# When the first weights are loaded and converted in a fused attention and two-MLP kernel: order of the first loads, grain of v, one more conversion tile

## The chip, the cores and the metric

The kernel runs on one core of one Trainium2 chip. The metric is the time of one execution on the device in microseconds (us), as a median of several runs. Engines are named as in the profile: PE (TensorE; PEld is its weight load), DVE (VectorE), ACT (ScalarE), POOL (GpSimd) and SP (SyncE, which issues most DMAs).

## What is computed

Attention inside chunks of 64 positions (4 batches, 8 heads, 576 positions, 64 per head), then an MLP with squared ReLU, then a second MLP of four experts that are mixed by probabilities:

```python
scores = scale * np.matmul(q_c, k_c.transpose(0, 1, 2, 4, 3))
attn = np.exp(scores - max); attn = attn / (sum + 1e-09)
x = np.matmul(attn, v_c)                    # as 2304 tokens of 512
h = np.maximum(x @ w_in, 0.0)               # w_in 512 x 2048
x = h * h @ w_out                           # w_out 2048 x 512
h = np.maximum(x @ w1[e], 0.0)              # e = 0 to 3, 512 x 1024
out += p[:, e:e + 1] * (h @ w2[e])
```

`w_in` and `w_out` come as 64-bit floats, seen by the kernel as pairs of 32-bit words; everything else is 32-bit.

## The kernel before, in words

**Precision.** The MLP products take 32-bit operands as a rounded half (`hi`) and a remainder (`lo`): three matmuls for one product. So each weight tile and each tile of x is split by ACT (the rounding copy) and POOL or DVE (the subtraction).

**Ticks.** The order of all instructions is written out by hand: the loop over `r` (L659) records one tick after another, and each engine works through its own queue in that order. Tick r of the first 20 handles token tile r of 128 tokens (18 tiles) in a staggered way: scores of tile r on PE (`s1_stage`, L233) and their maxima and differences on DVE (L239, L240); the normalisation of tile r-1 on DVE (`norm_stage`, L251 to L254); the transposes of the attention weights of tile r-2 (`s2_stage`, L260), of q and of k of tile r+1 (`s0_stage`, L218, copied out by ACT at L222); the product with v for tile r-2 (`s3_stage`, L274) and its split into x (ACT L281, DVE L282). From tick 5 on (`LEAD`) the first MLP runs between these: step m = r-5 of `l1` (x @ w_in, 12 matmuls at L298, then ACT L308, DVE L309, ACT L311, DVE L312) and step m-1 of `l2` (12 matmuls at L328). A step takes one of four 128-wide pieces f of the hidden layer for one block of tokens; tiles 0 to 2 are the first block.

**Units.** A unit (n, which) is one 512 KB tile of `w_in` (which 0) or `w_out` (which 1) for piece n. It is loaded into one of four `raw` tiles (L108, L113), converted from 64 bits to 32 (ACT L125, L126; DVE L127, L130, and after a pause L135, L138; POOL L139, L140) into a tile `cv`, of which there are three (`CV_BUFS`), and split in a later tick (ACT L151, POOL L152), which frees the `cv` tile. `FIRST` gives the ticks in which the first eight units are converted, `FIRST_LOAD` those in which they are loaded; their order is (0,0), (1,0), (0,1), (2,0), (1,1), (3,0), (2,1), (3,1).

**Loads.** Before tick 0 the q, k of tiles 0 and 1 and two chunks of v are loaded, by SP and ACT. After that each tick's loads are recorded at its start: `do(r, "load")` calls each job, where a unit's load is issued at once, and `merge` takes the others (generators) in turn, one DMA of each. q and k of tile r+2 are due in tick r, v of batch b as a whole in tick 9b/2 - 1, on SP; k of tile 2 alone is issued by ACT. Each DMA takes the next of eight semaphores and waits for the transfer that last used that semaphore; the rows of the order below name them DMAHW0 to DMAHW7.

Of the kernel before, what the change touches and what calls it, by code (L numbers as in the profile page):

```python
# [13 lines left out]
ALU = mybir.AluOpType  # L14
# [11 lines left out]
LEAD = 5  # L26
QK_BUFS = 3
ACC_EARLY = 3
FIRST = [2, 3, 4, 4, 5, 6, 6, 7]
FIRST_LOAD = [0, 1, 2, 2, 3, 4, 5, 5]  # L30
WARM = 8
SECOND = [-3, -2, -1, 1, 2, 3, 4, 5]
RAW_BUFS = 4
CV_BUFS = 3
HALF = 384
NSUP = 3
SWAP = 63
# [9 lines left out]
def tile_kernel(ctx, tc, q, k, v, moe_w_in, moe_w_out, moe2_p, moe2_w1, moe2_w2, out):  # L47
    nc = tc.nc
# [3 lines left out]
    E, _, F2 = moe2_w1.shape  # L52
# [3 lines left out]
    NCB = S // CH  # L56
# [48 lines left out]
    def unit_load(n, which):  # L105
        r = rawp.tile([P, DM, 2], I32, tag="raw", name="raw")
        if which == 0:
            nc.sync.dma_start(  # L108
                out=r.rearrange("p (k f) w -> p k (f w)", k=KD),
                in_=moe_w_in[:, 2 * n * P:2 * (n + 1) * P].rearrange("(k p) f -> p k f", p=P),  # L110
            )
        else:
            nc.sync.dma_start(  # L113
                out=r.rearrange("p f w -> p (f w)"), in_=moe_w_out[n * P:(n + 1) * P, :]
            )
        raw[n, which] = r

    def unit_convert(n, which):

# [171 lines left out]
    def l1(i):  # L291
        p, tb, f = steps[i]
        T = BLOCKS[tb]
        ah, al = halves[p * G + f, 0]
        ph = bank("h" if "w" not in late else "httt")
        for kk in range(KD):
            for n, (w, x) in enumerate(((ah, xh), (ah, xl), (al, xh))):
                nc.tensor.matmul(  # L298
                    ph[:, :T], lhsT=w[:, kk, :], rhs=x[tb][:, kk, :],
                    start=(kk == 0 and n == 0), stop=(kk == KD - 1 and n == 2),  # L300
                )
            if kk < KD - 1:
                yield
        o = GP_AT + i % (LAG + 1) * 1024
        hi, lo = ar[:, o:o + 512], ar[:, o + 512:o + 1024]
        gh[i], gl[i] = hi, lo
        r = rp.tile([P, 512], F32, tag="r", name="r")
        nc.scalar.activation(out=r[:, :T], in_=ph[:, :T], func=AF.Relu)  # L308
        nc.vector.tensor_tensor(out=r[:, :T], in0=r[:, :T], in1=r[:, :T], op=ALU.mult)  # L309
        yield  # L310
        nc.scalar.copy(hi[:, :T], r[:, :T])  # L311
        nc.vector.tensor_tensor(  # L312
            out=lo[:, :T], in0=r[:, :T], in1=hi[:, :T].bitcast(F32), op=ALU.subtract
        )
# [251 lines left out]
    def at(tick, kind, fn, *args):  # L566
        jobs[kind].setdefault(max(0, tick), []).append((fn, args))

    def do(tick, kind):
        return [fn(*args) for fn, args in jobs[kind].pop(tick, ())]  # L570

    for t in range(2, NTILE):
        at(t - 2, "load", load_qk, t, (nc.sync, nc.scalar if t == 2 else nc.sync))
    for b in range(B):
        if b == 0:
            for c in (2, 3):
                at(0, "load", load_v_chunk, b, c, (nc.sync, nc.sync))
            at(1, "load", load_v, b, 4, NCB)
        else:
            at(b * NCB // 2 - 1, "load", load_v, b, 0, NCB)  # L580
    order = [(0, 0), (1, 0), (0, 1), (2, 0), (1, 1), (3, 0), (2, 1), (3, 1)]
    for p in range(npass1):
        for u, (f, which) in enumerate(order):
            if p == 0:
                tick = FIRST[u]
            elif p == 1:
                tick = NTILE + LAG_A + SECOND[u]
            else:
                tick = LEAD + (p - 1) * G * NB + UOFF[u]
            unit = (p * G + f, which)  # L590
            at(FIRST_LOAD[u] if p == 0 else tick - 2, "load", unit_load, *unit)
            at(tick, "convert", unit_convert, *unit)
            at(max(tick + 1, NTILE + LAG_A if p == 1 else 0), "split", unit_split, *unit)
    def merge(loads):
        loads = [y for y in loads if hasattr(y, "__next__")]
        while loads:
            loads = [y for y in loads if next(y, loads) is not loads]

    with tc.manual_schedule():
        ident = const.tile([P, P], F32, name="ident")  # L600
# [1 line left out]
        warm = bank("t")  # L602
        for _ in range(WARM):
            nc.tensor.matmul(warm[:, :P], lhsT=ident, rhs=ident, start=True, stop=True)
        two = (nc.sync, nc.scalar)
        merge([load_qk(0, two)])
        merge([load_qk(1, two)])
        for c in range(2):
            merge([load_v_chunk(0, c, two)])
        dp = const.tile([P, NTILE, E], F32, name="dp")  # L610
        psum_ = const.tile([P, NTILE, 1], F32, name="psum_")
        prob = const.tile([P, NTILE, E], F32, name="prob")
# [46 lines left out]
        for r in range(LEAD + NS + LAG):  # L659
            m = r - LEAD  # L660
            tags = "ttthaaaa" if m < 0 else "t"
            ch = mlp(m) if m >= 0 else iter(())
            if r == NTILE + LAG_A:
                att.close()
                late["x"] = ctx.enter_context(tc.tile_pool(name="xq", bufs=1, side="right"))
                late["w"] = lw.enter_context(tc.tile_pool(name="wpb", bufs=RING_B, side="right"))
            merge(do(r, "load"))
            if r < NTILE + LAG_A:
                if r < NTILE:
                    s1_stage(r, tags)  # L670
                if 0 <= r - 1 < NTILE:
                    norm_stage(r - 1)
                conv = do(r, "convert")
                for c in conv:
                    next(c)
                run(ch, 3)
                if 0 <= r - LAG_A:
                    s2_stage(r - LAG_A, tags)
                if r + 1 < NTILE:
                    s0_stage(r + 1, tags, 0)  # L680
                run(ch, 2)
                if r + 1 < NTILE:
                    s0_stage(r + 1, tags, 1)
                for c in conv:
                    run(c)
                run(ch, 1)
                if 0 <= r - LAG_A:
                    s3_stage(r - LAG_A, tags)
                if r < NTILE:
                    exp_stage(r)  # L690
                do(r, "split")
            else:
                if r == SWAP:
                    staging.close()
                    late["raw"] = ctx.enter_context(tc.tile_pool(name="raw", bufs=1, reuse_waits="tile"))
                for fn, args in early.pop(r, ()):
                    fn(*args)
                if r > y0_at:
                    next(late.setdefault("y0", y_combine(0)), None)
                if m < NS:  # L700
                    run(ch, KD + 2)
                    conv = do(r, "convert")
                    for c in conv:
                        next(c)
                    run(ch, 1)
                    for c in conv:
                        run(c)
                    do(r, "split")
            if m < NS:
                run(ch)  # L710
# [68 lines left out]
```

## Time and profile before

| | |
|---|---|
| median of 3 runs | 1264.28 us (1263.84 to 1265.97) |
| the profiled execution | 1261.85 us, span 1260.1 us |
| PE busy | 1231.7 us, 98% of the span |
| PEld busy | 1090.4 us, 87% |
| POOL busy | 628.8 us, 50% |
| DVE busy | 705.0 us, 56% |
| ACT busy | 521.3 us, 41% |
| PE in the first two of 40 slices | 6 and 7 tenths; 9 tenths in all others but the last |
| DMA in the first two of 40 slices | 209 and 197 GB/s; 68 GB/s over the span |

A busy PE is not a PE at its peak, since its matmuls are pipelined and their ends are modelled. The idle time of an engine counts only where the work that ended last ran through it: the chain of waits tells where that was.

### The profile page before, as it was taken

What the parts mean: (1) busy time and instruction counts of PE and PEld (TensorE: products, weight loads), DVE (VectorE), ACT (ScalarE), POOL (GpSimd) and SP (SyncE); (2) the same over time, 40 slices, a digit from 0 to 9 for tenths busy, and PEclk for the clock granted to TensorE, in tenths of its full rate; (3) what the DMA queues carried; (4) which work ended last, traced back from release to release, by engine and by line L of the source; (5) the groups of instructions that cost most, each with busy time, mean ns of one, the idle gap of its engine ahead of it and who ended that gap; (6) DMA issues with size and microseconds to landing.
All of it is one profiled execution on the core that took longest, in us unless ns stands there. A gap on an engine that the chain in (4) does not pass through costs nothing.

```text
span 1260.1 us, 18090 instructions
## 1 busy us (share of the span) xinstructions
PE 1231.7 (98%) x7048; PEld 1090.4 (87%) x7048; DVE 705.0 (56%) x1135; ACT 521.3 (41%) x934; POOL 628.8 (50%) x507
## 2 busy tenths in 40 slices
PE   6799999999999999999999999999999999999998
PEld 5688788988988988888888888888888888888887
DVE  4876667755765355355555573555555735555555
ACT  3654455432432223633333355333333553333331
POOL 0530046431432022766776686767766866666650
PEclk7889999999999999999999999999999999999999
DMA  9947012210201000222222223222222232222211
GB/s 209 197 77 168 5 51 87 66 51 17 67 1 50 1 1 17 67 67 68 67 67 67 68 76 109 68 69 70 69 69 70 66 122 68 70 67 69 67 35 66
DMA packets 136838, 87.19 MB, mean 69 GB/s; under 512 B 62769, under 2 KB 120113, under 8 KB 136753
## 3 DMA queue, kind: packets, MB, share of 16 engines
q1 hardware_dynamic: 133088, 85.12, 24.9%
q10 hardware_dynamic: 3664, 0.92, 0.4%
q8 instruction: 55, 0.90, 0.3%
q14 instruction: 31, 0.25, 0.1%
HBM read 81.30 MB, written 4.72 MB: 68 GB/s over the span
## 4 chain that ended last, share of the span: by engine, by line
PE 91%; DVE 3%; ACT 1%; issue 0%; POOL 0%; DVEq 0%
PE psa L543 32%; PE pst L498 24%; PE psa L328 14%; PE pst L298 9%; PE psh L298 6%; PE psh L498 4%; PE pst L274 1%; PE pst L233 1%; PE pst L218 1%; DVE cv L127 0%; PE pst L260 0%; DVE r L309 0%; DVE cv L130 0%; DVE ar L312 0%; DVE cv L135 0%
## 5 line engine op out<-in xcount | busy, mean ns | idle before, releaser
L543 PE MATMUL psa<-ar 128*128 128x512 f32 x1728 | 445.7, 393 | 0.0
L543 PEld LDWEIGHTS psa<-ar 128*128 128x128 f32 x1728 | 320.0, 188 | 50.3
L466 POOL TENSOR_TENSOR ar<-raw,ar 128x896 fp32r<-128x896 f32 x96 | 204.2, 2129 | 274.4 <-ACT ar L465 274.4
L498 PE MATMUL pst<-ar 128*128 128x384 f32 x1728 | 339.2, 335 | 0.9 <-ACT u L507 0.9
L498 PEld LDWEIGHTS pst<-ar 128*128 128x128 f32 x1728 | 307.3, 188 | 22.8 <-ACT u L507 1.6
L556 DVE SCALAR_TENSOR_TENSOR o<-psa,prob,o 128x512 f32<-128x512 f32 x270 | 201.5, 747 | 173.4 <-PE psa L543 173.4
L139 POOL TENSOR_TENSOR raw<-raw 128x512 f32<-128x512 f32 x32 | 36.2, 1131 | 230.0 <-DVE raw L138 97.6
L456 POOL TENSOR_TENSOR raw<-raw 128x256 f32<-128x256 f32 x192 | 141.3, 754 | 8.8 <-DMA raw<-in_moe_w 5.2
L475 POOL TENSOR_TENSOR ar<-raw,ar 128x512 fp32r<-128x512 f32 x96 | 123.4, 1306 | 12.5 <-ACT ar L474 12.5
L309 DVE TENSOR_TENSOR r<-r 128x512 f32<-128x512 f32 (+1 forms) x80 | 64.9, 811 | 108.9 <-ACT r L308 108.8
L328 PE MATMUL psa<-ar 128*128 128x512 f32 (+1 forms) x480 | 114.7, 379 | 1.3 <-POOL ar L152 1.2
L507 ACT COPY u<-pst 128x384 f32<-128x384 f32 x96 | 46.0, 479 | 163.8 <-PE pst L498 163.8
L511 ACT ACTIVATE ar<-pst 128x384 fp32r<-128x384 f32 x96 | 47.2, 492 | 149.7 <-DVE pst L532 116.3
L328 PEld LDWEIGHTS psa<-ar 128*128 128x128 f32 x480 | 87.6, 191 | 14.3 <-POOL ar L152 1.5
L328 PE MATMUL psa<-ar,h 128*128 128x512 f32 (+1 forms) x320 | 93.7, 373 | 1.6 <-ACT ar L311 0.8
L511 ACT ACTIVATE ar<-psh 128x384 fp32r<-128x384 f32 x96 | 47.2, 492 | 109.8 <-DVE psh L521 78.6
L465 ACT CAST ar<-raw 128x896 fp32r<-128x896 f32 x96 | 90.1, 939 | 0.0
L312 DVE TENSOR_TENSOR ar<-r,ar 128x512 fp32r<-128x512 f32 (+1 forms) x80 | 61.6, 770 | 39.9 <-ACT ar L311 39.1
L512 DVE SCALAR_TENSOR_TENSOR ar<-psh,ar 128x384 fp32r<-128x384 f32 x96 | 53.5, 558 | 53.6 <-ACT ar L511 53.6
L311 ACT CAST ar<-r 128x512 fp32r<-128x512 f32 (+1 forms) x80 | 46.1, 577 | 71.0 <-DVE r L309 71.0
L512 DVE SCALAR_TENSOR_TENSOR ar<-pst,ar 128x384 fp32r<-128x384 f32 x96 | 53.5, 557 | 31.2 <-ACT ar L511 29.1
L298 PE MATMUL pst<-ar,h 128*128 128x512 f32 (+1 forms) x240 | 69.3, 370 | 0.0
(106 smaller groups left out, 1482.9 us busy)
## 6 DMA issues: line engine op xcount, KB each, us to landing
raw<-in_moe_w SPq DMA_DIRECT2D x48, 512.0 KB, 3.9
raw<-in_moe_w SPq DMA_DIRECT2D x48, 256.0 KB, 3.0
raw<-in_moe_w SPq DMA_DIRECT2D x96, 128.0 KB, 3.0
raw<-in_moe_w_in SPq DMA_DIRECT2D x16, 512.0 KB, 3.8
raw<-in_moe_w_out SPq DMA_DIRECT2D x16, 512.0 KB, 3.7
out<-o SPq DMA_DIRECT2D x18, 256.0 KB, 3.2
q<-in_q SPq DMA_DIRECT2D x16, 256.0 KB, 4.7
v<-in_v SPq DMA_DIRECT2D x24, 144.0 KB, 4.5
```

Of the source, the lines that this page charges most:

```text
L298: nc.tensor.matmul(ph[:, :T], lhsT=w[:, kk, :], rhs=x[tb][:, kk, :], start=(kk == 0 and n == 0), stop=(kk == KD - 1 and n == 2),)
L309: nc.vector.tensor_tensor(out=r[:, :T], in0=r[:, :T], in1=r[:, :T], op=ALU.mult)
L328: nc.tensor.matmul(o, lhsT=w, rhs=y, start=(f == 0 and n == 0), stop=(f == G - 1 and n == 2))
L456: nc.gpsimd.tensor_tensor(out=r[:, o], in0=r[:, a], in1=r[:, b], op=op)
L465: nc.scalar.copy(h, a)
L466: nc.gpsimd.tensor_tensor(out=l, in0=a, in1=h.bitcast(F32), op=ALU.subtract)
L475: nc.gpsimd.tensor_tensor(out=l, in0=a, in1=h.bitcast(F32), op=ALU.subtract)
L498: nc.tensor.matmul(p, lhsT=w[:, kk, :], rhs=y[:, kk, :], start=(kk == 0 and z == 0 and u in (0, 1, 3)), stop=(kk == 1 and z == 2 and u in ...
L511: nc.scalar.activation(out=h, in_=p, func=AF.Relu)
L512: nc.vector.scalar_tensor_tensor(out=l, in0=p, scalar=0.0, in1=h.bitcast(F32), op0=ALU.max, op1=ALU.subtract)
L543: nc.tensor.matmul(p, lhsT=w[:, ts], rhs=y[:, i, :], start=(i == 0 and z == 0), stop=(i == 1 and z == 2))
L556: nc.vector.scalar_tensor_tensor(out=o, in0=p, scalar=pe, in1=o, op0=ALU.mult, op1=ALU.add)
```

## The change

Six edits; line numbers in the changed kernel are higher by 3 to 9.

1. Units (0,0) and (1,0) are loaded by SP before tick 0, between q of tile 0, q of tile 1 and v.
2. Unit u of the first eight is converted in tick u (before: 2, 3, 4, 4, 5, 6, 6, 7), split in the tick after, and loaded in tick u-2.
3. A unit's load becomes a generator too, and `run_all` issues the loads of a tick one job after the other instead of in turns: q and k, then v, then the unit.
4. v of batch 0 comes chunk by chunk (two chunks a tick), v of the others in two parts, four chunks and five, each later by one tick or more. SP issues k of tile 2.
5. There are four `cv` tiles instead of three.
6. The square in `l1` is computed by DVE as max(ph, 0) * r from the PSUM tile `ph` and ACT's result r, instead of r * r.

```diff
-FIRST = [2, 3, 4, 4, 5, 6, 6, 7]
-FIRST_LOAD = [0, 1, 2, 2, 3, 4, 5, 5]
+FIRST = [0, 1, 2, 3, 4, 5, 6, 7]
-CV_BUFS = 3
+CV_BUFS = 4
...
+    def unit_load_later(n, which):
+        unit_load(n, which)
+        yield
...
-        nc.vector.tensor_tensor(out=r[:, :T], in0=r[:, :T], in1=r[:, :T], op=ALU.mult)
+        nc.vector.scalar_tensor_tensor(
+            out=r[:, :T], in0=ph[:, :T], scalar=0.0, in1=r[:, :T], op0=ALU.max, op1=ALU.mult
+        )
...
-        at(t - 2, "load", load_qk, t, (nc.sync, nc.scalar if t == 2 else nc.sync))
+        at(t - 2, "load", load_qk, t)
     for b in range(B):
         if b == 0:
-            for c in (2, 3):
-                at(0, "load", load_v_chunk, b, c, (nc.sync, nc.sync))
-            at(1, "load", load_v, b, 4, NCB)
+            for c in range(2, NCB):
+                at(c // 2 - 1, "load", load_v_chunk, b, c, (nc.sync, nc.sync))
         else:
-            at(b * NCB // 2 - 1, "load", load_v, b, 0, NCB)
+            at(b * NCB // 2, "load", load_v, b, 0, NCB // 2)
+            at((b * NCB + NCB // 2) // 2, "load", load_v, b, NCB // 2, NCB)
...
-            at(FIRST_LOAD[u] if p == 0 else tick - 2, "load", unit_load, *unit)
+            if tick > 1:
+                at(tick - 2, "load", unit_load_later, *unit)
...
-    def merge(loads):
-        loads = [y for y in loads if hasattr(y, "__next__")]
-        while loads:
-            loads = [y for y in loads if next(y, loads) is not loads]
+    def run_all(loads):
+        for y in loads:
+            if hasattr(y, "__next__"):
+                for _ in y:
+                    pass
...
-        merge([load_qk(0, two)])
-        merge([load_qk(1, two)])
-        for c in range(2):
-            merge([load_v_chunk(0, c, two)])
+        run_all([load_qk(0, two)])
+        unit_load(*order[0])
+        run_all([load_qk(1, two)])
+        unit_load(*order[1])
+        run_all([load_v_chunk(0, c, two) for c in range(2)])
...
-            merge(do(r, "load"))
+            run_all(do(r, "load"))
```

The DMA queue of SP from its start, before (`in_moe_w_in` and `in_moe_w_out` are units; a q or k tile is 128x8x64, a v chunk two DMAs of 64x4x64):

```order
L184 DMA q<-in_q 128x8x64 x2
L207 DMA v<-in_v 64x4x64 x2
L108 DMA raw<-in_moe_w_in 128x4x256
L184 DMA q<-in_q 128x8x64
L207 DMA v<-in_v 64x4x64 x4
L108 DMA raw<-in_moe_w_in 128x4x256
L184 DMA q<-in_q 128x8x64
L196 DMA v<-in_v 64x5x64 x2
L184 DMA k<-in_k 128x8x64
L196 DMA v<-in_v 64x5x64 x6
L113 DMA raw<-in_moe_w_out 128x1024
L108 DMA raw<-in_moe_w_in 128x4x256
```

And in the changed kernel, up to the unit that tick 1 loads:

```order
L187 DMA q<-in_q 128x8x64
L107 DMA raw<-in_moe_w_in 128x4x256
L187 DMA q<-in_q 128x8x64
L107 DMA raw<-in_moe_w_in 128x4x256
L210 DMA v<-in_v 64x4x64 x2
L187 DMA q<-in_q 128x8x64
L187 DMA k<-in_k 128x8x64
L210 DMA v<-in_v 64x4x64 x4
L112 DMA raw<-in_moe_w_out 128x1024
L187 DMA q<-in_q 128x8x64
L187 DMA k<-in_k 128x8x64
L210 DMA v<-in_v 64x4x64 x4
```

Two units now stand ahead of v and one of them ahead of q of tile 1; q and k of a tile stand together, and the rest of v no longer lies between them.

The queue of ACT in ticks 0 and 1, before, with the semaphores that each row waits for (L222 copies q and k, L246 is the exponential, L125 opens a conversion):

```order
L222 COPY kT<-pst 128x512 [waits PE_49]
L184 DMA k<-in_k 128x8x64 [waits DMAHW0_49]
L222 COPY qT<-psa 128x512 [waits PE_49]
L222 COPY kT<-psa 128x512 [waits PE_49]
L246 ACTIVATE e<-e 128x512 [waits DVE_49]
L222 COPY qT<-pst 128x512 [waits PE_49,Activation_49]
```

And in the changed kernel (L225 and L249 are those lines, L128 opens a conversion):

```order
L225 COPY kT<-pst 128x512 [waits PE_49]
L128 ACTIVATE cv<-raw 128x512 [waits DMAHW3_49]
L129 ACTIVATE raw<-raw 128x512
L225 COPY qT<-psa 128x512 [waits PE_49]
L225 COPY kT<-psa 128x512 [waits PE_49]
L249 ACTIVATE e<-e 128x512 [waits DVE_49]
L128 ACTIVATE cv<-raw 128x512 [waits DMAHW7_49]
L129 ACTIVATE raw<-raw 128x512
L225 COPY qT<-pst 128x512 [waits PE_49,Activation_49]
```

The issue of k of tile 2 has left ACT's queue. In its place, ahead of the copies of tile 1, stands the first conversion, which waits for unit (0,0); the second stands ahead of the copies of tile 2.

## Rows read from the trace of the kernel before

**Rows 1.** By stage: stretch, length, busy PE, PEld, DVE, ACT, POOL; clock, DMA share, GB/s.

```profile
0.00:2.00 2.00, 0.66 (x3) 0.66 (x4) 0.00 (x0) 0.00 (x0) 0.68 (x6) 1.00 0.03 8
...
20.00:40.00 20.00, 12.82 (x222) 11.37 (x224) 17.60 (x41) 11.83 (x22) 6.25 (x6) 0.84 1.08 205
40.00:58.00 18.00, 13.59 (x149) 12.23 (x146) 15.55 (x30) 9.99 (x20) 11.03 (x9) 0.84 0.97 220
90.00:500.00 410.00, 408.18 (x2464) 352.83 (x2461) 244.16 (x390) 161.74 (x291) 113.82 (x86) 1.00 0.16 45
```

**Rows 2.** The chain of waits, 0 to 160 us: start us, us, what.

```profile
74.94 1.49 PE psh L298 x7
...
76.86 0.44 PE pst L218 x4
...
81.67 0.91 PE pst L233 x30
...
89.74 0.91 PE pst L233 x30
```

**Rows 3.** ACT in order of time: start us, us, what, idle before and its releaser.

```profile
11.27 0.58 ACT L222 COPY qT<-psa 128x512 f32<-128x512 f32 x1 [4.30 <-DMA raw<-in_moe_w_in]
```

**Rows 4.** Who waited for whom, 0 to 76 us: us in total, times, longest.

```profile
ACT cv L125 <- POOL ar L152: 14.4, 4, 6.1
```

**Rows 5.** The same for DVE alone, 9.7 to 75.3 us.

```profile
DVE mx L239 <- PE psa L233: 4.3, 1, 4.3
...
DVE r L309 <- ACT r L308: 2.1, 2, 1.0
DVE ar L312 <- ACT ar L311: 2.0, 2, 1.3
```

**Rows 6.** DVE in order of time, ticks 3 and 4.

```profile
27.45 0.68 DVE L251 TENSOR_REDUCE sm<-e 128x8 f32<-128x512 f32 x1
...
29.22 0.42 DVE L127 TENSOR_SCALAR cv<-cv 128x512 f32<-128x512 f32 x1
...
30.13 0.69 DVE L135 SCALAR_TENSOR_TENSOR cv<-raw,cv 128x512 int32<-128x512 int32 x1
30.86 0.43 DVE L138 TENSOR_SCALAR raw<-cv 128x512 int32<-128x512 int32 x1
32.86 0.69 DVE L282 TENSOR_TENSOR ar<-psa,ar 128x512 fp32r<-128x512 f32 x1 [1.58 <-ACT ar L281]
33.47 0.41 DVE L239 TENSOR_REDUCE mx<-psa 128x4 f32<-128x256 f32 x1
...
35.05 0.68 DVE L251 TENSOR_REDUCE sm<-e 128x8 f32<-128x512 f32 x1
```

**Rows 7.** DVE's squares (L309; min/median/max ns) and an operation like the new one (L512).

```profile
L309 DVE TENSOR_TENSOR r<-r x80: 546/691/1779, 48.7 to 499.2; 128x512 f32<-128x512 f32 x48, 128x384 f32<-128x384 f32 x32
...
L512 DVE SCALAR_TENSOR_TENSOR ar<-psh,ar 128x384 fp32r<-128x384 f32 x96 | 53.5, 558 | 53.6 <-ACT ar L511 53.6
```

**Rows 8.** DVE and POOL in order of time, tick 5.

```profile
51.60 1.29 POOL L140 TENSOR_TENSOR cv<-cv,raw 128x512 f32<-128x512 f32 x1
...
51.66 1.65 DVE L312 TENSOR_TENSOR ar<-r,ar 128x384 fp32r<-128x384 f32 x1 [0.72 <-ACT ar L311]
```

**Rows 9.** PE in order of time, ticks 4 to 6.

```profile
37.51 0.65 PE L218 MATMUL pst<-ident,k 128*128 128x128 f32 x4 [3.44 <-DMA k<-in_k]
...
39.07 1.53 PE L233 MATMUL pst<-kT,qT 64*64 64x64 f32 x31
41.99 3.25 PE L298 MATMUL psh<-ar 128*128 128x384 f32 x9 [1.38 <-DVE ar L282]
...
50.12 1.83 PE L298 MATMUL psh<-ar 128*128 128x384 f32 x9
```

**Rows 10.** Busy time by stage, the stretch of half clock in tick 5.

```profile
39.10:45.90 6.80, 5.42 (x52) 5.13 (x47) 6.57 (x12) 1.62 (x3) 6.05 (x5) 0.50 1.11 239
```

**Rows 11.** POOL's longest operation of a conversion: ns min/median/max, first and last start.

```profile
L140 POOL TENSOR_TENSOR cv<-cv,raw x8: 1282/1301/1371, 26.6 to 72.4; 128x512 f32<-128x512 f32 x8
```

## The prediction

> **What bounds the kernel now.** I read the stages first. From 90 us on PE is busy 408.18 of 410 us at full clock [rows 1]; before that it is not: 12.82 of 20 us between 20 and 40 us, 13.59 of 18 between 40 and 58, at a mean clock of 0.84, while DVE works 17.60 of 20 and 15.55 of 18 us and the DMA share is about 1 at 205 to 220 GB/s. So there are two kernels: a start in which PE waits, and a rest in which PE sets the time. The chain of waits puts the border at 74.94 us: from there on it is PE without a gap, and the ticks follow each other at 89.74 - 81.67 = 8.07 us [rows 2]. Whatever makes tick 9 begin earlier than 81.67 us (its first scores on PE) is carried to the end, because everything behind is PE's own work. That one number is what I forecast.
>
> Three things hold the start back. ACT stood 4.30 us before the copies of tile 1, behind the issue of k of tile 2, which waited for the first unit's transfer [rows 3]; DVE stood 4.3 us for tile 1's scores in consequence [rows 5]. ACT waited 14.4 us in four pieces, up to 6.1 us, to begin a conversion, because all three `cv` tiles were taken until POOL had split one [rows 4]; behind that stand the copies of q and k, ReLU and cast of the same tick, and DVE waited 2.1 and 2.0 us for the last two [rows 5]. And in tick 5 PE ran at half clock: 5.42 us of work between 39.1 and 45.9 us [rows 10], where nine matmuls took 3.25 us that take 1.83 at full clock [rows 9].
>
> **The change, part by part.**
>
> *k of tile 2 leaves ACT, conversions move to ticks 0 to 7.* The 4.30 us stop goes. In its place ACT waits for unit (0,0) ahead of tile 1's copies, and so on tick by tick. A unit that tick r converts stands in the DMA queue ahead of q of tile r+1, whose copies it precedes on ACT, so it is there first and costs ACT only its two instructions. What is late next is the transfer itself. Bytes ahead of a tile's end: 0.524 MB for each tile's q and k, 0.524 for each unit, 0.131 for each chunk of v. Tile 5 ends after 6 tiles, 5 units and 8 chunks, 6.81 MB; at 0.205 MB/us [rows 1] and a start at 2 us (up to then next to nothing moves [rows 1]) that is 35.2 us, against k of tile 5 at 37.51 us now [rows 9]. Tile 8 ends after 9 tiles, 8 units and 13 chunks, 10.6 MB: 53.8 us. From k's arrival to tile 5's scores were 39.07 - 37.51 = 1.6 us [rows 9], and the scores take 0.9 [rows 2]: DVE can take up tile 5 at 35.2 + 2.5 = 37.7 us. By then five conversions lie behind it instead of four.
>
> *Ticks 5 to 7.* DVE's work in a tick, from [rows 6]: scores 35.05 - 33.47 = 1.58; normalisation 29.22 - 27.45 = 1.77; conversion 30.13 - 29.22 = 0.91 and 30.86 + 0.43 - 30.13 = 1.16; x 33.47 - 32.86 = 0.61. The square is 0.55 at its shortest [rows 7], and I take the same for the remainder. Sum 7.1 us. POOL's conversions run beside it: L312 began 0.06 us after L140 of POOL and took 1.65 us, ending 0.42 us after POOL's end, 1.1 more than its shortest [rows 8]. I add 0.7 a tick, between nothing and that. So 7.8 us in tick 5, and in ticks 6 and 7 PE's pace of 8.07 is the longer one. DVE takes up tile 6 at 45.5, tile 7 at 53.6, tile 8 at 61.7 us; transfers are ahead from tile 6 on. In tick 8 PE's q transposes wait for the first half of the scores on DVE (0.8), and from there to tick 9 are 81.67 - 76.86 = 4.81 us [rows 2]: tick 9 at 67.3 us.
>
> *Clock.* PE still idles in ticks 1 to 4, so I keep one stretch of 6.8 us at half clock on the path, as in tick 5 now [rows 10]: 3.4 us. Bounds: none, or two of them. Tick 9 at **70.7 us, 11.0 us earlier**.
>
> *Four `cv` tiles.* Now a `cv` tile is written again four units later, when its split is two ticks old: the 14.4 us of [rows 4] go. This is what lets ticks 5 to 7 run at the sum above. If the cover went (POOL more than two ticks behind), the wait of up to 6.1 us would be back.
>
> *v in chunks and halves.* 26 more DMAs on SP, 2 for batch 0 and 8 for each other batch; later units are also moved past q, k and v of their tick. Nobody waits for SP in the chain of waits. v is loaded two ticks before it is used, 16 us at 8.07 a tick, and a unit likewise: nothing. If that cover were gone, PE would stop for what is missing of one transfer in a tick.
>
> *The square from PSUM.* 558 ns for an operation of that kind and size against 546 at the shortest now [rows 7]: nothing in the start; later the mean falls, off the path. PE's next step must now wait until DVE has read `ph`, where ACT's ReLU sufficed: a rival.
>
> **Sum.** The profiled execution took 1261.85 us, so 1261.85 - 11.0 = 1250.9; the median of the runs stands 2.4 above it, which gives **1253.3 us**. Ends: no half clock, and transfers at 220 GB/s [rows 1] (tile 5 at 33.0, 2.2 earlier): 1247.7. Half clock twice: 1256.7.
>
> **Rivals.**
>
> *The units stop ACT after all.* The eight semaphores make each DMA wait for the eighth before it, so a unit can be issued late; then ACT stands before the copies as it did once, for 4.3 us [rows 3]. Once on the path: 1257.6. For it: two units now precede v of tile 0, and the transfers are full. Against it: the order puts each unit ahead of the tile that it could stop.
>
> *The one bank of `ph`.* Until tick 19 there is one PSUM bank for `l1`. If PE waits 0.5 us for DVE's square in each of 15 ticks, 7.5 us go: about 1261. It decides where DVE lags the tick by more than the PE work between two steps; in a tick the second layer's twelve matmuls, two transposes and two attention products lie between, so I give it little.
>
> *POOL holds DVE up (slower).* POOL's three operations on a unit take up to 1.3 us each [rows 11], 3.9 a tick, now in every tick from 0 to 8. If each held DVE up for its whole length, a tick would be 3.2 us longer than I reckon; in ticks 2 to 7 that is 19.2 us, tick 9 at 89.9, slower than now: **1272.5**. The point from which it decides: 0.7 + 11.0 / 6 = 2.5 us lost a tick. For it speaks [rows 8]; against it that this row shows 1.1 us in the tick with the longest such operation. The Trainium skill, page "SBUF — State Buffer", section "SBUF: two separate sides", says that DVE and GpSimd share one pair of ports as an exclusive lock, that a DVE instruction needs it with two SBUF inputs or in a 2-port mode, and that the loser blocks for the whole instruction. By it this rival would be the upper end, and the new square, with one input in PSUM, would be out of it. The trace agrees as far as L312 ended 0.42 us after POOL did; no row shows what share of POOL's operations meets such an instruction.
>
> *It changes nothing.* Tiles no earlier and DVE as late as now: 1264. Against it: both ACT stops end by construction.
>
> **How the numbers follow.** Forecast 0.62 (1248 to 1257), units stop ACT 0.16, one bank 0.09, POOL 0.06, nothing 0.04, earlier than my low end 0.03. Range 1247.5 to 1260: it takes in the forecast's ends and the first rival and leaves out about 0.2. A measurement of this kernel can tell 0.2%, 2.5 us, from no change: faster 0.86 (forecast, first rival, low end, half of the bank's), within 0.2% 0.08, slower 0.06.
>
> **What would show it.** In the changed profile ACT should not wait for a `cv` split (now 14.4 us) nor 4 us for a unit; DVE should take up tile 5 near 38 us and tile 8 near 62 to 65; the scores of tick 9 should begin on PE at 67 to 74 us, the ticks behind it last 8.07 us. Wrong would be: ACT waits of several us for units; DVE operations beside POOL over 1 us in every tick; PE idle before `l1`'s first matmul for DVE's square; or a start shorter by 11 us and a time that is not, which would mean that the rest is not PE's alone.

## The result and the profile after

The changed kernel takes **1248.32 us** (median of 4 runs, 1247.99 to 1248.79) against 1264.23 us (1263.84 to 1265.97, 4 runs beside it): ratio 0.9877 [0.9865, 0.9889], 15.9 us faster. Forecast were 1253.3 us in a range of 1247.5 to 1260. The profiled execution took 1248.07 us, its span is 1246.2 us, 13.9 less than before.

Line numbers are those of the changed kernel now: scores L236, their maxima and differences L242 and L243, normalisation L254 to L257, transposes L221, conversions L128 and L129 (ACT), L130 to L141 (DVE), L142 and L143 (POOL), splits L154 and L155, x L284 and L285, `l1` L301, ReLU L311, square L312, its split L316 and L317, `l2` L333.

Busy time by stage, the stretches of [rows 1], columns as there:

```profile
20.00:40.00 20.00, 14.09 (x225) 11.68 (x224) 19.21 (x39) 12.31 (x23) 10.82 (x10) 0.76 0.94 199
40.00:58.00 18.00, 17.34 (x215) 15.83 (x214) 16.76 (x37) 12.55 (x24) 9.98 (x8) 1.00 0.78 177
90.00:500.00 410.00, 407.77 (x2377) 352.95 (x2376) 227.00 (x382) 163.50 (x290) 114.90 (x91) 1.00 0.16 45
```

PE is fuller between 40 and 58 us (17.34 of 18 us instead of 13.59), at full clock. Between 20 and 40 us DVE is: 19.21 of 20. The chain of waits (start us, us, what), where [rows 2] showed tick 9 at 81.67:

```profile
27.94 6.70 DMA k<-in_k
34.65 0.04 issue
...
48.17 0.63 PE pst L221 x4
...
69.23 0.91 PE pst L236 x30
...
77.32 0.91 PE pst L236 x30
```

k of tile 5 lands at 34.65 us. From 48.17 us on the chain is PE's alone, where before it was from 74.94. Tick 9 begins on PE at 69.23, 12.4 us earlier; the ticks behind are as long as before (77.32 - 69.23 = 8.09, then 7.93). The weight loads of the second MLP's first layer (min/median/max ns, then first and last start in us), in the kernel before:

```profile
L498 PEld LDWEIGHTS pst<-ar x1728: 186/188/189, 500.9 to 1247.5; 128*128 128x128 f32 x192
```

and in the changed kernel:

```profile
L503 PEld LDWEIGHTS pst<-ar x1728: 186/188/189, 487.0 to 1233.6; 128*128 128x128 f32 x192
```

So 13.9 us are won there: 12.4 up to tick 9, and 1.5 between tick 9 and the end of the first MLP. From there on the two run alike (1247.5 - 500.9 = 746.6 us and 1233.6 - 487.0 = 746.6 us).

Some of ACT's waits from 0 to 76 us (the longest and the one for units), where [rows 4] had 14.4 us for `cv` tiles and [rows 3] 4.30 for a unit:

```profile
ACT aT L265 <- PE pst L263: 7.3, 4, 2.4
...
ACT kT L225 <- PE pst L221: 4.1, 5, 2.0
...
ACT cv L128 <- DMA raw<-in_moe_w_out: 0.9, 2, 0.6
```

No wait for a split is left, and for units ACT waits 0.9 us in all. DVE's waits from 9.7 to 75.3 us, against [rows 5]:

```profile
DVE ar L317 <- ACT ar L316: 2.1, 4, 0.8
DVE mx L242 <- PE psa L236: 1.6, 1, 1.6
DVE ar L285 <- ACT ar L284: 1.5, 1, 1.5
```

DVE in order of time in tick 4 (start us, us, what), and beside it POOL:

```profile
32.36 0.42 DVE L242 TENSOR_REDUCE mx<-psa 128x4 f32<-128x256 f32 x1
...
33.94 0.68 DVE L254 TENSOR_REDUCE sm<-e 128x8 f32<-128x512 f32 x1
34.65 0.97 DVE L255 TENSOR_SCALAR sm<-sm 128x8 f32<-128x8 f32 x1
...
36.50 0.42 DVE L130 TENSOR_SCALAR cv<-cv 128x512 f32<-128x512 f32 x1
...
39.09 0.42 DVE L242 TENSOR_REDUCE mx<-pst 128x4 f32<-128x256 f32 x1
```

```profile
34.33 1.26 POOL L155 TENSOR_TENSOR ar<-cv,ar 128x512 fp32r<-128x512 f32 x1
```

DVE has no pause in this tick. Its addition on 8 columns (L255) lasts 0.97 us and ends at 35.62, right behind POOL's split at 35.59; free of POOL it takes 172 ns.

When DVE takes up each tile (first L242 of it, L239 in the kernel before, us) shows where each kernel gains or loses. The last two columns are the start of tick 9 on PE, from the chain of waits, and the time of the profiled execution. The experiments in the rows are told further below; e7 and e11 carry the main finding.

| tile | 1 | 2 | 3 | 4 | 5 | 6 | 7 | 8 | tick 9 | time |
|---|---|---|---|---|---|---|---|---|---|---|
| before | 14.04 | 19.93 | 25.87 | 33.47 | 41.85 | 53.23 | 63.24 | 75.22 | 81.67 | 1261.85 |
| after | 13.37 | 18.71 | 25.61 | 32.36 | 39.09 | 47.20 | 54.54 | 63.26 | 69.23 | 1248.07 |
| e3, old v | 12.36 | 18.76 | 25.08 | 36.34 | 42.28 | 50.43 | 57.76 | 66.48 | 72.45 | 1251.36 |
| e4, k2 on ACT | 16.70 | 22.03 | 28.94 | 35.69 | 42.43 | 53.24 | 60.56 | 69.27 | 75.24 | 1254.17 |
| e7, edits 1 to 3 | 16.42 | 21.76 | 28.66 | 35.40 | 42.18 | 52.22 | 59.54 | 68.25 | 74.21 | 1254.45 |
| e9, fill | 13.41 | 18.75 | 27.24 | 33.22 | 39.94 | 48.06 | 55.38 | 64.10 | 70.07 | 1248.98 |
| e10, pairs | 13.24 | 18.58 | 25.49 | 30.25 | 38.63 | 47.85 | 57.70 | 65.76 | 71.70 | 1250.73 |
| e11, old ticks | 12.43 | 18.48 | 24.41 | 30.35 | 39.55 | 50.67 | 60.54 | 69.89 | 77.87 | 1256.65 |
| e12, POOL remainder | 13.27 | 18.65 | 25.99 | 32.28 | 39.03 | 46.15 | 55.27 | 63.20 | 70.20 | 1248.68 |

The gain is not made while the first tiles arrive: at tile 4 it is 1.1 us. It is made from there on: ticks 5 to 7 of the kernel before were 3.3, 2.7 and 3.3 us longer. Against the changed kernel, e3, e4, e9, e10 and e11 lose in the time what they lose by the start of tick 9, within 0.2 us (e12 0.4 less, and e7, with the old square, 1.4 more); so what decides lies ahead of tick 9. A start is not the same twice: two kernels that differ from the changed one only later on, e2 and e8, take up tile 1 at 12.1 us instead of 13.37, and yet begin tick 9 at 69.25 and 69.30.

### The profile page after: what moved, and what is told of

The parts are those of the page before. It is cut to its first block, busy times and chain, and to the rows that moved or that the text cites. A ratio compares the mean times of both kernels' runs of the same rounds, so it can differ in the third digit from the quotient of the medians.

```text
span 1246.2 us, 18128 instructions
## 1 busy us (share of the span) xinstructions
PE 1228.4 (99%) x7048; PEld 1088.0 (87%) x7048; DVE 687.5 (55%) x1135; ACT 522.7 (42%) x934; POOL 621.7 (50%) x507
## 4 chain that ended last, share of the span: by engine, by line
PE 94%; DVE 3%; DMA 1%; ACT 1%; issue 0%; SPq 0%; DVEq 0%; ACTq 0%
PE psa L548 32%; PE pst L503 24%; PE psa L333 15%; PE pst L301 9%; PE psh L301 6%; PE psh L503 4%; PE pst L277 1%; PE pst L221 1%; PE pst L236 1%; DMA q<-in_q 1%; DMA k<-in_k 1%; PE pst L263 0%; DVE cv L130 0%; DVE cv L133 0%; DVE cv L138 0%
## 5 line engine op out<-in xcount | busy, mean ns | idle before, releaser
L142 POOL TENSOR_TENSOR raw<-raw 128x512 f32<-128x512 f32 x32 | 33.3, 1041 | 228.3 <-issue 103.9
L512 ACT COPY u<-pst 128x384 f32<-128x384 f32 x96 | 46.0, 479 | 163.7 <-PE pst L503 163.7
L333 PE MATMUL psa<-ar 128*128 128x512 f32 (+1 forms) x480 | 112.8, 375 | 0.1
L333 PEld LDWEIGHTS psa<-ar 128*128 128x128 f32 x480 | 86.3, 188 | 12.6 <-DVE ar L317 0.4
L333 PE MATMUL psa<-ar,h 128*128 128x512 f32 (+1 forms) x320 | 93.2, 372 | 1.1 <-ACT ar L316 0.8
L317 DVE TENSOR_TENSOR ar<-r,ar 128x512 fp32r<-128x512 f32 (+1 forms) x80 | 60.6, 757 | 39.4 <-ACT ar L316 37.8
L312 DVE SCALAR_TENSOR_TENSOR r<-pst,r 128x512 f32<-128x512 f32 (+1 forms) x48 | 30.7, 640 | 71.2 <-ACT r L311 71.2
L311 ACT ACTIVATE r<-pst 128x512 f32<-128x512 f32 (+1 forms) x48 | 26.7, 557 | 102.8 <-PE pst L301 102.1
L301 PE MATMUL pst<-ar,h 128*128 128x512 f32 (+1 forms) x240 | 69.3, 370 | 0.0
```

Source lines behind the costliest of these rows:

```text
L301: nc.tensor.matmul(ph[:, :T], lhsT=w[:, kk, :], rhs=x[tb][:, kk, :], start=(kk == 0 and n == 0), stop=(kk == KD - 1 and n == 2),)
L317: nc.vector.tensor_tensor(out=lo[:, :T], in0=r[:, :T], in1=hi[:, :T].bitcast(F32), op=ALU.subtract)
L333: nc.tensor.matmul(o, lhsT=w, rhs=y, start=(f == 0 and n == 0), stop=(f == G - 1 and n == 2))
```

## Experiments

Each changed kernel is compared with runs of the kernel before on the same chip, so the ratios stand beside 0.9877 [0.9865, 0.9889].

### e1: three `cv` tiles

```diff
-CV_BUFS = 4
+CV_BUFS = 3
```

> The changed kernel with three cv tiles again. Theory A, that of the prediction: the fourth tile is what lets ticks 5 to 7 run; then ACT waits for POOL's splits again (14.4 us of such waits before) and the time goes back by 3 to 8 us, to 1251 to 1256. Theory B: the waits came from ticks with two conversions (4 and 6); with one a tick, unit u needs the tile of unit u-3, whose split is recorded two ticks earlier, so nothing waits and the time stays within 1 us of 1248.3.

Measured: 1248.57 us, ratio 0.9885 [0.9872, 0.9899], the time of the changed kernel. ACT waits for no split here either. That is theory B: the fourth tile carries nothing once conversions are early and one to a tick.

### e2: the old square

```diff
-        nc.vector.scalar_tensor_tensor(
-            out=r[:, :T], in0=ph[:, :T], scalar=0.0, in1=r[:, :T], op0=ALU.max, op1=ALU.mult
-        )
+        nc.vector.tensor_tensor(out=r[:, :T], in0=r[:, :T], in1=r[:, :T], op=ALU.mult)
```

> The changed kernel with the square as r * r again. Theory A: the 1.4 us that the changed kernel gains behind tick 9 (PE's waits for DVE's remainder and the order around 185 to 215 us) come from the shorter, undisturbed square: 1249 to 1250.5. Theory B: the square is off the path everywhere: 1248.3 within 0.7, and the 1.4 us belong to loads or to POOL.

Measured: 1249.84 us, 0.9898 [0.9883, 0.9913]; by the times alone this hardly differs from the changed kernel. The trace places it: tick 9 begins on PE at 69.25 us (69.23 after), and the second MLP begins 1.6 us later than after:

```profile
L501 PEld LDWEIGHTS pst<-ar x1728: 186/188/189, 488.6 to 1235.2; 128*128 128x128 f32 x192
```

So the square is what wins the 1.5 us behind tick 9 (theory A). PEld's largest waits for the split of the square between 76 and 490 us in this kernel (`l2` is L331 here):

```profile
PEld psa L331 <- DVE ar L315: 2.1, 5, 0.6
PEld psa L331 <- ACT ar L314: 1.7, 3, 1.2
```

In the changed kernel they are 1.2 us each (69 to 490 us):

```profile
PEld psa L333 <- DVE ar L317: 1.2, 3, 0.4
PEld psa L333 <- ACT ar L316: 1.2, 1, 1.2
```

The new operation's duration shows why (min/median/max ns; one row for each kind of PSUM tile); [rows 7] had 546/691/1779:

```profile
L312 DVE SCALAR_TENSOR_TENSOR r<-psh,r x32: 549/688/692, 44.1 to 485.3; 128x512 f32<-128x512 f32 x18, 128x384 f32<-128x384 f32 x14
L312 DVE SCALAR_TENSOR_TENSOR r<-pst,r x48: 543/691/692, 169.1 to 479.8; 128x512 f32<-128x512 f32 x30, 128x384 f32<-128x384 f32 x18
```

Minimum and median are the old ones; the lengthened instances are gone.

### e3: v loaded as before

```diff
-            for c in range(2, NCB):
-                at(c // 2 - 1, "load", load_v_chunk, b, c, (nc.sync, nc.sync))
+            for c in (2, 3):
+                at(0, "load", load_v_chunk, b, c, (nc.sync, nc.sync))
+            at(1, "load", load_v, b, 4, NCB)
...
-            at(b * NCB // 2, "load", load_v, b, 0, NCB // 2)
-            at((b * NCB + NCB // 2) // 2, "load", load_v, b, NCB // 2, NCB)
+            at(b * NCB // 2 - 1, "load", load_v, b, 0, NCB)
```

> The changed kernel with v loaded as before (chunks 2 and 3 in tick 0, the rest of batch 0 in tick 1, other batches whole, a tick earlier). Theory A: bytes ahead of a tile set when it comes; 2 to 3 chunks more stand ahead of tiles 3 and 4 and about 1.2 MB more of batch 1 ahead of tiles 6 and 7, at 0.2 MB/us 1 to 2 us for tile 4 and up to 5 us for tile 6, of which DVE's own pace hides a part: 1250 to 1253. Theory B: DVE's work sets ticks 3 to 8 and transfers do not matter: 1248.3 within 1.

Measured: 1252.85 us, 0.9916 [0.9903, 0.993]: 4.5 us are lost by the medians, 3.3 by the profiled executions; theory A. ACT's longest wait is now for a unit,

```profile
ACT cv L128 <- DMA raw<-in_moe_w_in: 7.5, 2, 4.3
```

and PE's is 5.9 us for q: five chunks of v at once stand on SP's queue in tick 1 ahead of the next unit and the next q. Tile 4 is taken up 4.0 us late, and 3.2 of it stay. From tile 5 on the ticks are as in the changed kernel, so the loss shown is that of batch 0; nothing is seen to be lost by loading the v of batch 1 whole.

### e4: k of tile 2 issued by ACT

```diff
-        at(t - 2, "load", load_qk, t)
+        at(t - 2, "load", load_qk, t, (nc.sync, nc.scalar if t == 2 else nc.sync))
```

> The changed kernel with k of tile 2 issued by ACT again. Theory A: ACT stops before the copies of tile 1 until the semaphore that this transfer takes is free, 2 to 5 us, and the start is later by 1 to 4 us: 1249.5 to 1252. Theory B: DVE has the first conversion to do in that time and the stop is made up for by tick 3: 1248.3 within 1.

Measured: 1253.13 us, 0.9923 [0.9911, 0.9936]: 4.8 us are lost, 1.1 more than theory A allowed. ACT in order of time, with idle time before and its releaser:

```profile
12.82 0.66 ACT L128 ACTIVATE cv<-raw 128x512 f32<-128x512 f32 x1 [5.38 <-DMA v<-in_v]
```

The stop of [rows 3] is back, 5.38 us now; its releaser is a transfer of v. Every tile from 1 to 5 comes 3.3 us late. At tile 6 it is 6.0: PE stood 4.34 us before tick 5's `l1` and then ran it at half clock,

```profile
42.57 3.25 PE L301 MATMUL psh<-ar 128*128 128x384 f32 x9 [4.34 <-DVE ar L285]
```

so the tick took 53.24 - 42.43 = 10.81 us instead of 8.11. Most of that second part is the clock's as I read it (DVE waits 1.23 and 0.76 us for ReLU and cast there). In e3 `l1` of tick 5 begins at nearly the same time, at 42.42 us, its nine matmuls take 1.83 us, and the tick takes 8.15; but e3 differs in more than the clock, and a fill in this kernel was not tried. The profiled execution is the slowest of the five, 1.0 us above their median.

### e5 and e6: one edit alone in the kernel before

e5 gives the kernel before a fourth `cv` tile, e6 issues its k of tile 2 by SP:

```diff
-CV_BUFS = 3
+CV_BUFS = 4
```

> The kernel before with four cv tiles alone. Theory A: ACT's 14.4 us of waits for POOL's splits are a part of the loss by themselves; with the fourth tile they fall below 5 us and the time by 3 to 8 us, to 1255 to 1260. Theory B: ACT waits there for work that is late anyway, since two conversions stand in ticks 4 and 6 and DVE and POOL must do them; then the waits go from ACT to the next engine and the time stays within 2 us of 1263.4.

```diff
-        at(t - 2, "load", load_qk, t, (nc.sync, nc.scalar if t == 2 else nc.sync))
+        at(t - 2, "load", load_qk, t)
```

> The kernel before with k of tile 2 issued by SP, alone. Theory A: the ACT stop costs what it cost in the run that put it back into the changed kernel, 4 to 5 us: 1258.4 to 1259.4. Theory B: behind it, from tick 4 on, the ticks with two conversions and the wait for cv tiles set the pace whenever they begin, and most of it is lost again by tick 8: 1261 to 1263.4.

Measured: e5 1261.45 us, 0.9979 [0.9969, 0.9988]; e6 1264.17 us, 1.0 [0.9991, 1.0009]. Both are nearer to theory B: e5 gains 2.6 us against the kernel before beside it (1264.07), e6 nothing, a little less than theory B left it. In e5 the 14.4 us of waits for splits fall to one of 1.06, and only 2.6 us come of it, because ACT now waits elsewhere:

```profile
ACT aT L262 <- PE pst L260: 10.3, 3, 4.8
```

In e6 DVE takes up tile 1 at 10.56 us (14.04 before) and tile 3 at 24.16, but tile 4 at 34.84 (33.47 before): the early gain runs into the transfers, as PE shows in order of time (q of tile 4, then k of tile 5).

```profile
28.75 1.09 PE L218 MATMUL psh<-ident,q 128*128 128x128 f32 x4 [3.63 <-DMA q<-in_q]
...
37.60 0.66 PE L218 MATMUL pst<-ident,k 128*128 128x128 f32 x4 [1.58 <-DMA k<-in_k]
```

### e7: edits 1 to 3 alone

The changed kernel with four things as in the kernel before: three `cv` tiles, the old square, the old loads of v, k of tile 2 on ACT (the diffs of e1 to e4 together). What is left is the early, single conversions and the order of the loads.

> The kernel before with edits 1, 2 and 3 alone (two units ahead of tick 0, conversions one a tick from tick 0, a unit's load behind its tick's q, k and v); three cv tiles, old square, old v, k of tile 2 on ACT. Theory A: the parts add up; put back one by one, square, v and this issue cost 1.3, 4.3 and 4.6 us, so of 15 us about 5 are left for the order of the conversions: 1257.5 to 1260. Theory B: with two units ahead of it the issue on ACT and the whole v make tiles 1 to 4 later than in the kernel before, and these edits alone are worth less than 2 us: 1261.5 to 1265.

Measured: 1254.3 us, 0.9919 [0.9905, 0.9933]: 9.8 us faster than before, more than theory A's 4 to 6 and outside both theories. That is so although ACT's waits are long; none of them is for a split, with three `cv` tiles:

```profile
ACT cv L128 <- DMA raw<-in_moe_w_in: 7.9, 2, 4.7
ACT cv L128 <- DMA v<-in_v: 5.8, 1, 5.8
```

DVE is later than in the kernel before at tiles 1 to 5 and 7.0 us earlier at tile 8. (By the two profiled executions the gain is 7.4 us; that of the kernel before lay 2.4 us below its median.)

### e8: one tiny operation less

This kernel leaves out the 1e-9 that is added to the softmax sum.

```diff
-        nc.vector.tensor_scalar_add(sm, sm, 1e-9)
         nc.vector.reciprocal(sm, sm)
```

> The changed kernel without the addition of 1e-9 to the sums of the softmax (left out: one DVE operation on 128 x 8 numbers a tick, which in ticks 3 to 5 took 1.0 us beside POOL instead of 0.17). Theory A: DVE is the bound of ticks 2 to 6 and POOL's hold on it costs what it shows, so 0.2 to 1.0 us a tick go, 2 to 4 us in all: 1244.5 to 1246.5. Theory B: POOL's hold only moves to the next operation that it can stop (the product L257), and what is left is the operation's own 0.2 us in some five ticks: 1247 to 1248.3.

Measured: 1248.38 us, 0.9876 [0.9862, 0.9889], no gain, nearest to theory B. In ticks 3 and 5 the delay goes to the next operation but one, the product e*sm, which takes 0.69 us free of POOL:

```profile
26.70 1.28 DVE L256 TENSOR_TENSOR e<-e,sm 128x512 f32<-128x512 f32 x1
...
41.30 1.31 DVE L256 TENSOR_TENSOR e<-e,sm 128x512 f32<-128x512 f32 x1
```

That is not all of it. Ticks 4 and 5 are shorter on DVE, 5.74 and 7.67 us instead of 6.73 and 8.11, so that tile 6 comes at 46.45 us, 0.75 earlier than in the changed kernel. Then a transfer takes this back: in tick 6 PE waits for q of tile 7.

```profile
47.99 0.63 PE L221 MATMUL pst<-ident,q 128*128 128x128 f32 x4 [1.17 <-DMA q<-in_q]
```

The same transposes begin at 48.17 us in the changed kernel. SP issues this q at 42.52 us, behind a unit and eight DMAs of v, which take its queue from 34.79 us on. So the next limit stood close behind DVE.

### e9: PE kept busy in ticks 2 to 4

```diff
+        def fill(n, tags):
+            w = bank(tags)
+            for _ in range(n):
+                nc.tensor.matmul(w[:, :P], lhsT=ident, rhs=ident, start=True, stop=True)
...
+                if 2 <= r <= 4:
+                    fill(8, tags)
                 if r + 1 < NTILE:
                     s0_stage(r + 1, tags, 0)
+                if 2 <= r <= 4:
+                    fill(4, tags)
```

> The changed kernel with twelve matmuls more (identity by identity, 128x128, into a bank that nobody reads) in each of ticks 2 to 4, so that PE idles less there; the output is the same. The changed kernel ran its stretch of half clock from 33.4 to 40.2 us. Theory A: that stretch lies on the path, as the prediction's clock term had it (3.4 us). If the fill takes it away, tick 9's scores begin 2 to 3.4 us earlier than 69.16 us and the time falls to about 1245 to 1246. Theory B: DVE sets the pace there (46.3 us busy of 49.6), so full clock saves only what DVE waits for PE, 0 to 0.5 us: 1247.8 to 1248.6, also where the granted clock is 1.0 from 33 to 40 us. If the stretch of half clock stays, the run says nothing of either, and the time is 1248 to 1250.

Measured: 1249.38 us, 0.9888 [0.9875, 0.9902]. The fill did what it should. The changed kernel between 32 and 40 us (columns as in [rows 1]):

```profile
32.00:36.00 4.00, 1.97 (x12) 1.40 (x14) 3.83 (x9) 1.79 (x5) 3.52 (x3) 0.65 0.77 189
36.00:40.00 4.00, 3.83 (x66) 3.64 (x65) 3.86 (x9) 2.73 (x6) 1.22 (x2) 0.50 1.09 205
```

The kernel with the fill:

```profile
32.00:36.00 4.00, 4.00 (x60) 3.93 (x56) 3.86 (x9) 3.63 (x7) 3.13 (x3) 1.00 1.01 245
36.00:40.00 4.00, 3.06 (x73) 2.57 (x71) 3.83 (x9) 2.81 (x6) 0.89 (x2) 1.00 0.89 171
```

From 4 us of half clock and more to none, and DVE steps from tile 4 to 5 in 39.94 - 33.22 = 6.72 us and from 5 to 6 in 8.12, where the changed kernel took 6.73 and 8.11. DVE, busy 3.83 to 3.86 of 4 us in both, does not notice. PE waits 1.02 us for DVE's x there instead of 0.17. The one us that the kernel loses is lost by tile 4: tile 3 comes 1.63 us late (27.24 instead of 25.61), with the fill ahead of its scores, and 0.86 of that are left at tile 4. That is theory B's mechanism; the time lies 0.8 us above its range, about what the fill itself costs. An earlier stretch of half clock, from about 10 to 23 us, is in the changed kernel and in this one alike, so nothing is shown of its cost.

### e10 and e11: other ticks for the conversions

Both are the changed kernel; e11 keeps its first two loads ahead of tick 0. A unit is loaded two ticks ahead of its conversion, so some loads move too: those of two units in e10, of four in e11.

```diff
-FIRST = [0, 1, 2, 3, 4, 5, 6, 7]
+FIRST = [0, 1, 2, 4, 4, 5, 6, 6]
```

> The changed kernel with the first eight units converted in ticks 0, 1, 2, 4, 4, 5, 6, 6: early, but with two conversions in ticks 4 and 6 and none in 3 and 7, which were the pairs of the kernel before. Four cv tiles stay. Theory A: one conversion a tick is what counts; with pairs ACT waits again several us for a split, or DVE's tick with two conversions (9 us) is on the path, and the time rises by 2 to 5 us, 1250 to 1253. Theory B: what counts is that two conversions are done before tick 2, when DVE and ACT are idle for transfers; the sum of DVE's work to tick 8 is the same, so DVE takes up tile 8 within 1 us of 63.26 us and the time stays at 1248 to 1249.

```diff
-FIRST = [0, 1, 2, 3, 4, 5, 6, 7]
+FIRST = [2, 3, 4, 4, 5, 6, 6, 7]
...
-            if tick > 1:
+            if p > 0 or u > 1:
```

> The changed kernel with the first eight units converted in the ticks of the kernel before (2, 3, 4, 4, 5, 6, 6, 7), all else as changed: the first two units still loaded before tick 0, v in chunks, four cv tiles, the new square. Theory A: the work of the conversions, put behind tick 2, is what costs: two conversions of 2.1 us on DVE fall into ticks 4 to 7 where DVE has no room, so tick 9 comes 4 to 6 us later and the time is 1252 to 1255. Theory B: the early ticks alone carry nearly all of the gain (11 to 13 us), because the pairs in ticks 4 and 6 also stop ACT: 1257 to 1262. Theory C: the order of the loads carries it, not the ticks: 1248 to 1250.

Measured: e10 1251.61 us, 0.9911 [0.9896, 0.9926], 3.3 us slower than the changed kernel; e11 1257.24 us, 0.9947 [0.9934, 0.9959], 8.9 slower. In e10 the tick with the second pair takes 57.70 - 47.85 = 9.85 us instead of 7.34. In e11 every tick from 5 to 7 takes 9 to 11 us, at half clock in tick 5 again (nine matmuls of `l1` in 3.25 us), and in tick 8 PE waits for a split:

```profile
71.14 1.49 PE L301 MATMUL psh<-ar 128*128 128x384 f32 x7 [1.76 <-POOL ar L155]
```

Theory A for e10; for e11 the size of theory B, but its reason only in part: among ACT's waits to 76 us there is one of 1.0 us for a `cv` tile (14.4 us in the kernel before) and 1.5 us for units, and the time goes in DVE's ticks, the clock and that split. Tiles 1 to 4 come earlier in e11 than in the changed kernel, so its loads do not hold the start back.

### e12: POOL takes the remainder

```diff
-        nc.vector.tensor_tensor(
+        (nc.gpsimd if i < 3 else nc.vector).tensor_tensor(
             out=lo[:, :T], in0=r[:, :T], in1=hi[:, :T].bitcast(F32), op=ALU.subtract
         )
```

> The changed kernel with the remainder of the hidden tile (r minus its rounded half, 128x384) computed by POOL instead of DVE in the first three steps of the first MLP, ticks 5 to 7. DVE spent 2.8 us on these three and 1.4 us before them. Theory A: DVE sets the pace there, so 2 to 4 us of its time come off the path until PE's own pace of about 8 us takes over; with tile 6 at 47.20 and tile 7 at 54.54 us the ticks 5 to 7 are at that pace already in two of three, so 1 to 2.5 us are left: 1245.8 to 1247.4. Theory B: POOL is late (its conversions and splits stand ahead in its queue) and the second layer's matmuls wait for the remainder, or its operations hold DVE up as long as they save: 1248 to 1251.

Measured: 1248.8 us, 0.9883 [0.987, 0.9897], nothing gained, theory B. DVE takes up tile 6 1.05 us earlier (46.15), but POOL's operations hold up two of its next ones:

```profile
48.44 0.99 DVE L255 TENSOR_SCALAR sm<-sm 128x8 f32<-128x8 f32 x1
...
49.70 1.22 DVE L257 TENSOR_TENSOR e<-e,sm 128x512 f32<-128x512 f32 x1
```

```profile
48.13 1.27 POOL L155 TENSOR_TENSOR ar<-cv,ar 128x512 fp32r<-128x512 f32 x1
49.35 1.02 POOL L317 TENSOR_TENSOR ar<-r,ar 128x384 fp32r<-128x384 f32 x1
```

PE waits for q of tile 7 again, and 0.29 us for POOL's remainder; tile 7 is 0.7 us late.

```profile
48.81 0.63 PE L221 MATMUL pst<-ident,q 128*128 128x128 f32 x4 [1.72 <-DMA q<-in_q]
```

No version beat the changed kernel.

## Why the prediction was right, and where its steps were not

The border (PE alone decides behind tick 9), the sign and the range held. The sum came out 5.0 us too high, and three steps of it made that: tick 9 came at 69.2 instead of 70.7 us (1.5 us), 1.5 us more were won behind tick 9, and 2.2 us lie in the base: I added 2.4 us because the profiled execution of before was that much below its median, and the changed kernel's is only 0.25 below its own. (The parts are rounded, and the span fell by 13.9 us where the time of the execution fell by 13.8.) So no trace shows where these 2.2 of the 15.9 us lie. That the first part is so small is in part luck: the clock term and the late tile 5, below, are errors of opposite sign.

*Transfers: right for tile 5, with little to spare behind it.* Forecast 35.2 us for k of tile 5, measured 34.65. That "transfers are ahead from tile 6 on" held only just: where DVE came earlier (e8, e12), PE waited 1.17 and 1.72 us for q of tile 7.

*DVE's ticks 5 to 7: right in sum.* Forecast 7.8, 8.07, 8.07, together 23.9; measured 8.11, 7.34, 8.72, together 24.2. "In ticks 6 and 7 PE's pace of 8.07 is the longer one" is true of PE's chain, whose scores follow each other at 7.94 and 8.12 us from 53.17 us on; DVE's single ticks are not at it. But DVE took up tile 5 at 39.09 instead of 37.7, and not because of transfers: it had worked without a pause through tick 4, with 0.8 us for POOL in it.

*Clock: wrong.* "I keep one stretch of 6.8 us at half clock on the path ... 3.4 us." The stretch is there, 33.4 to 40.2 us, but it ends within the first microsecond of `l1` (39.23 us; nine matmuls in 2.19 us), and what DVE does beside it decides: e9 took it away and won nothing. It did cost where `l1` itself ran in it, as in tick 5 of the kernel before [rows 9, 10] and in e4 (up to 2.7 us for the tick, by the traces; no run took it away there). So part of the gain is, by the traces, a stretch of half clock that the change moved off tick 5's step. This error and the late tile 5 partly cancelled: DVE took up tile 8 at 63.26 instead of 61.7 us, 1.6 late, tick 9 began 6.0 instead of 5.6 us behind it, and the 3.4 us did not come.

*"Four `cv` tiles: this is what lets ticks 5 to 7 run": wrong.* e1 shows zero. By e1 and e7, conversions one a tick need only three tiles. So I read the waits of [rows 4] as those of two conversions in one tick (4 and 6), while an older unit was not yet split; no run has pairs, early, with three tiles. Nor were these waits the main cost: e5 removes nearly all of them and wins 2.6 us.

*What carries the gain* are, for the most part, the ticks of the conversions. e7 wins 9.8 us with edits 1 to 3 alone, and e11, which takes the ticks back (and with them the loads of four units), loses 8.9; it keeps 6.1 us of gain over the kernel before beside it (1263.36). No run has the ticks alone, without the new order of loads, so how the two share the 9.8 us of e7 is not shown. The prediction had this in its sum (five conversions behind tile 5 instead of four, no tick with two) but gave the credit to the tiles. The first conversions are done while transfers still arrive: ticks 0 to 3 hold four instead of two, ticks 4 to 7 four instead of six. The stretch from DVE's tile 4 to its tile 8 shows what that does (columns as in [rows 1]), before and after:

```profile
33.47:75.22 41.75, 31.53 (x365) 27.30 (x364) 35.33 (x67) 23.31 (x45) 23.48 (x20) 0.84 0.91 171
```

```profile
32.36:63.26 30.90, 28.39 (x367) 25.49 (x368) 28.38 (x60) 19.32 (x37) 17.04 (x15) 0.89 0.85 188
```

Of the 10.85 us won there DVE works 6.95 less and idles 3.9 less. Two conversions at 2.1 us are 4.2 of the 6.95; the rest is for the most part that fewer of its operations are drawn out (by the traces, 6.1 us above their shortest in these four ticks before, 3.0 after).

*"v in chunks and halves: nothing": wrong, by 3.3 us in the profiled executions and 4.5 in the medians.* The cover that I named (loads two ticks ahead) was true of v itself; I did not price what v delays on SP's queue when it comes at once, a unit and a q (e3).

*k of tile 2: right about the stop, wrong about its worth.* It is worth 4.8 us in the changed kernel (e4) and nothing in the kernel before (e6), where the later pairs and transfers take the gain back. The rival that the units stop ACT after all did not occur: 0.9 us in all to 76 us.

*The square: wrong by 1.5 us.* "Later the mean falls, off the path": it is on the path in a few steps behind tick 9 (e2). The rival of the one `ph` bank did not occur: of PE's waits from 69 to 490 us only two are listed, 0.8 and 0.3 us, both for the split of the square.

*POOL holds DVE: a real mechanism, far from its price.* It lengthens one or two of DVE's operations by 0.2 to 0.9 us in ticks 2 to 5 and 7 and none in tick 6, 0.8 us a tick on average, near the 0.7 that I took, not 3.2. e8 shows that taking one victim away wins nothing: in two ticks a later operation is held up instead, and what is left of the gain goes in a wait for a transfer. The Trainium skill, page "SBUF — State Buffer", section "SBUF: two separate sides", says that DVE needs the shared ports for two SBUF inputs or a 2-port mode, and that the loser blocks for the whole instruction. By that the new square, with one input in PSUM, is out of it; the trace agrees: at most 692 ns, where the old one reached 1779.

## What to carry to other kernels

Look for the engine that is busy nearly all the time in the stage that decides, and move its work to ticks where it waits for transfers anyway; the waits of other engines in that stage are partly its shadow, and removing them singly gave little here (2.6 us in e5, nothing in e6). The worth of an edit depends on the others (k of tile 2: nothing alone, 4.8 us with the rest): an early gain is kept only if every later tick can take it. Before an operation is taken off the engine that decides, look how close the next limit stands: in e8 and e12 it was a transfer that was due within about a microsecond. When transfers are the limit, count for each DMA what it stands ahead of, not only whether it is itself in time.

## What was not expected of the hardware

A stretch at half clock can cost nothing: 1.2 instead of 2.4 GHz for nearly 7 us, and the ticks around it are equal to 0.01 us (e9), while in the step that others wait for nine matmuls take 3.25 us instead of 1.83 and the tick was up to 2.7 us longer (e4). And an operation on 8 columns is held up for most of a 1.26 us POOL operation (0.97 instead of 0.17 us) while in the changed kernel no operation of DVE's L312, with one PSUM input, went above 0.69 us.
